# Forgetting attention and a gated convolution FFN on one core: two rewriting transfers taken out of each fill

## The chip, the core and the metric

The kernel runs on one core of a Trainium2 chip. The metric is device time in microseconds (us): the median of several executions. Beside it stands one execution that the hardware profiler recorded, with its own time and its span (first to last instruction). All views of the profile and of the trace are of that one execution. PE is the matmul engine, DVE the vector engine, ACT the scalar engine, POOL GpSimd; SP is the engine whose queue issues nearly all transfers here.

## What is computed

Attention with a forget gate over 8 batches, 8 heads, 576 positions and 64 elements per head, and then, on its output put back to (batch, position, 512), a feed-forward layer of width 1024 with a gate from a convolution over three positions.

```python
def _attn_ref(q, k, v, f):
    scores = scale * np.matmul(q, k.transpose(0, 1, 3, 2))
    cum = np.cumsum(np.log(np.clip(f, 0.0001, 1.0)), axis=-1)
    decay = cum[:, :, :, None] - cum[:, :, None, :]
    scores = np.where(causal, -1000000000.0, scores + decay)
    attn = softmax(scores)
    return np.matmul(attn, v)
...
def _moe_ref(x, w_in, conv_w, w_out):
    h = np.maximum(x @ w_in, 0.0)
    conv_out = conv_w[0] * h[s - 1] + conv_w[1] * h[s] + conv_w[2] * h[s + 1]
    gate = 1.0 / (1.0 + np.exp(-conv_out))
    return h * gate @ w_out
```

## The kernel before, in words

**Tiling.** The 64 pairs of batch and head are worked in 16 groups of four heads; group hb is half of batch hb // 2. For each group q and k are brought in turned, so that a tile `qk` holds 128 rows by 2 x 4 x 576 columns of bf16: the first half of the columns is q, the second is k. There are four such tiles (RING = 4), so group hb takes the tile of group hb - 4.

**Where the decay sits.** `load_qk` (L195 to L200) turns the fp32 inputs as pairs of 16-bit halves. The odd rows of the tile then hold the upper halves, which are the values in bf16; the even rows hold the lower halves, which aren't wanted. The kernel uses four of the even rows for the decay: row 0 of q holds the scaled cumulative sum and row 0 of k holds -1; rows 2 and 4 of q hold 1 and those of k hold the sum's upper part and its rest; row 6 is zero. One matmul over 128 rows then gives scores and decay together. All these rows for all heads are prepared once in `image`, a tensor in the chip's memory of shape (4 rows, 2 sides, 64 heads, 576): its decay parts are written by ACT's queue at L291, its constants by POOL's queue in `constants` (L293 to L295, task `zc`).

**How the even rows are set.** Groups 0 to 5 are cleared by DVE (`clamp`, L202), which also sets the constants; the decay rows follow by two transfers, `rows_of` (L217 to L220), for groups 1 to 5 (group 0 adds its decay by matmuls). For groups 6 to 15 it is done by transfers alone, in the task `fi{hb}`: `fill` (L211 to L215) writes zeros into 60 even rows (L212, 540 KB) and the image into the other four, both sides (L214, 36 KB), and `rows_of` then writes one row of q (L219, 4.5 KB) and two rows of k (L220, 9 KB) once more from the same places of the image. L219 writes bytes that L214 also writes, and is issued when L214 has landed.

**The order.** Nothing is scheduled while the kernel runs: `ORDER` (L17 to L67) is a list of tasks written out, and each engine takes its own tasks of it in that order. `add` gives each task its engine, what it must come after, and the buffers that it takes and gives back; waits between engines follow from the data. Tasks that the text names, by engine:

- SP: `q{hb}.0` and `q{hb}.1` load and turn q and k (L198); `fi{hb}` fills; `v{b}.{kb}` loads v of a batch in five parts (L226); `s{b}.{a}` stores a part of the output (L482, L485). From fill 6 on SP's order is fi6, v3.0, fi7, v3.2, fi9, v3.1, v3.4, v3.3, s0.2, s0.1, four parts of v4, s0.0, q8.0, q8.1, q10.1, q10.0, fi8, v4.4, fi10, s1.2, q11.1, q11.0, s1.0, fi11, v5, s2.0, q12, q13, fi12, s2.2, s1.1, fi13, s3.0, two parts of v7 and v6, q14, v6, s3.2, fi14, s4.0, v7, q15, s3.1, v7.4, fi15, and then stores.
- PE: `sd{i}` scores of the diagonal blocks of pair i (two heads; i // 2 is the group), `st{hb}` scores of the last 64 positions, `so{i}.{s}` the other scores (all with L316; a causal mask is added at L324 in groups 0 to 7), `pv{hb}.{u}` attention times v (L392), `t{hb}` turning (L408), `f{b}.{ff}` first FFN matmul (L422), `o{b}.{c}` second (L467, L471). All share four PSUM tiles.
- ACT: `ed`, `et`, `eo` the exponentials of the scores (L357, L336, L374), `r` relu (L432), `a` tanh (L456), `e{b}.{a}` copies of results from PSUM to one of three `ob` buffers (L477; some of them on DVE).
- DVE: `n` normalisation (L399, L400), `c` and `d` the convolution (L437, L439), `g` the gate (L460), `tx` copies after turning (L413, some on ACT). POOL: `va` casts of v (L233, L235), and `md`, `mt` the causal mask from group 8 on (L360, L339).

A group's score tasks come after its `fi` task. A `q` load comes after all score tasks of the group that had its tile before. A store's `ob` buffer can be taken again once the store has landed.

Of the kernel before, what the change touches and what calls it, by code (L numbers as in the profile page):

```python
# [69 lines left out]
class Plan:  # L70
# [8 lines left out]
    def add(self, name, engines, after, fn, take=(), give=(), behind=()):  # L79
        assert name not in self.tasks  # L80
        self.tasks[name] = dict(engines=engines.split("/"), after=[a for a in after if a], fn=fn, take=list(take),
                                give=list(give), behind=[a for a in behind if a])
        return name
# [21 lines left out]
def kernel(  # L105
# [83 lines left out]
    add = plan.add  # L189
# [5 lines left out]
    def load_qk(hb, h0, nh, side):  # L195
        t, src = ((stq_t, q), (stk_t, k))[side]
        t = t[hb % RING]
        nc.sync.dma_start_transpose(  # L198
            t.bitcast(U16)[:, h0 * S:(h0 + nh) * S],
            src[hb // 2, HH * (hb % 2) + h0:HH * (hb % 2) + h0 + nh].bitcast(U16).rearrange("h s d2 -> (h s) d2"))  # L200

    def clamp(hb, h0, nh, side):  # L202
        t = (stq_t, stk_t)[side][hb % RING].bitcast(U16)[:, h0 * S:(h0 + nh) * S]
        nc.vector.tensor_scalar(t, t, lim[:, 2 * side:2 * side + 1], lim[:, 2 * side + 1:2 * side + 2],
                                op0=ALU.mult, op1=ALU.add)

    def even_rows(hb, first, n, c0, c1):
        t, width = qk_t[hb % RING], 2 * HS + 64
        return bass.AP(tensor=t.tensor, offset=int(t.offset) + 2 * first * width + c0, ap=[[2 * width, n], [1, c1 - c0]])

    def fill(hb):  # L211
        nc.sync.dma_start(even_rows(hb, 4, 60, 0, 2 * HS).rearrange("p (h s) -> p h s", s=2 * S),  # L212
                          zero[0:60].unsqueeze(1).broadcast_to((60, HH, 2 * S)))
        nc.sync.dma_start(even_rows(hb, 0, 4, 0, 2 * HS).rearrange("j (a x) -> j a x", a=2),  # L214
                          image[:, :, hb * HH:(hb + 1) * HH, :].rearrange("j a h s -> j a (h s)"))  # L215

    def rows_of(hb):  # L217
        c = slice(hb * HH, (hb + 1) * HH)
        nc.sync.dma_start(even_rows(hb, 0, 1, 0, HS), image[0:1, 0, c, :].rearrange("j h s -> j (h s)"))  # L219
        nc.sync.dma_start(even_rows(hb, 1, 2, HS, 2 * HS), image[1:3, 1, c, :].rearrange("j h s -> j (h s)"))  # L220

    def load_v(b, kb):
        vf = vf_t[slot[f"v{b}.0", "vf"]]
        base = int(v.offset) + b * H * S * D
        n = 128 if kb < NKB - 1 else SL
        nc.sync.dma_start(vf[0:n, :, kb, :],  # L226
                          bass.AP(tensor=v.tensor, offset=base + kb * 128 * D, ap=[[D, n], [S * D, H], [1, D]]))

    def cast_v(hb, part):
        vf = vf_t[slot[f"v{hb // 2}.0", "vf"]][:, HH * (hb % 2):HH * (hb % 2 + 1)]  # L230
        va = va_t[slot[f"va{hb}.0", "va"]]
        if part == 0:
            nc.gpsimd.tensor_copy(va[:, :, 0:4, 0:D], vf[:, :, 0:4, :])  # L233
        else:
            nc.gpsimd.tensor_copy(va[0:SL, :, 4, 0:D], vf[0:SL, :, 4, :])  # L235
# [90 lines left out]
    def tail_scores(hb):  # L326
        on = hb in MASK_PE
        if on:
            masked(ps_of(f"st{hb}")[:, 0:HH * SL], HH, SL)
        for h in range(HH):  # L330
            scores(ps_of(f"st{hb}")[:, SL * h:SL * (h + 1)], hb, h, 512, 512, SL, m=SL, first=not on,
                   last=h == HH - 1 or not on)

    def tail_exp(hb):
        o = pt_t[slot[f"et{hb}", "pt"]][:, :, SL:128] if hb in MASK_PE else p3_t[slot[f"et{hb}", "p3"]]
        nc.scalar.activation(o, ps_of(f"st{hb}")[:, 0:HH * SL].rearrange("p (h j) -> p h j", j=SL), AF.Exp, scale=SCALE)  # L336
# [36 lines left out]
    def off_exp(i, s):  # L373
        nc.scalar.activation(pair(i)[:, s, 512:1536], ps_of(f"so{i}.{s}"), AF.Exp, scale=SCALE)  # L374
# [141 lines left out]
    for hb in range(NHB):  # L516
        b = hb // 2
        was = hb - RING
        old = [f"st{was}"] + [f"sd{2 * was + y}" for y in range(2)] + [
            f"so{2 * was + y}.{s}" for y in range(2) for s in range(2)] if was >= 0 else []  # L520
        if hb == 0:
            for p in range(2):
                add(f"cl0.{p}", "DVE", [], lambda p=p: [clamp(0, 2 * p, 2, side) for side in (1, 0)])
            ready = [["cl0.0"], ["cl0.1"]]
        else:
            for side in range(2):
                add(f"q{hb}.{side}", "SP", old, lambda hb=hb, side=side: load_qk(hb, 0, 4, side))
            if hb < NCL:
                for side in range(2):
                    add(f"cl{hb}.{side}", "DVE", [f"q{hb}.{side}"], lambda hb=hb, side=side: clamp(hb, 0, 4, side))  # L530
                add(f"rw{hb}", "SP", [f"cl{hb}.{side}" for side in range(2)], lambda hb=hb: rows_of(hb))
                ready = [[f"rw{hb}"]] * 2
            else:
                add(f"fi{hb}", "SP", [f"q{hb}.0", f"q{hb}.1", "zc"], lambda hb=hb: (fill(hb), rows_of(hb)))
                ready = [[f"fi{hb}"]] * 2
        if hb % 2 == 0:
            for kb in range(NKB):
                add(f"v{b}.{kb}", "SP", [], lambda b=b, kb=kb: load_v(b, kb), take=["vf"] if kb == 0 else [],
                    behind=[f"v{b}.0"] if kb else [])
        add(f"va{hb}.0", "POOL", [f"v{b}.{kb}" for kb in range(4)], lambda hb=hb: cast_v(hb, 0), take=["va"])  # L540
        add(f"va{hb}.1", "POOL", [f"v{b}.4"], lambda hb=hb: cast_v(hb, 1), behind=[f"va{hb}.0"],
            give=[("vf", f"v{b}.0")] if hb % 2 else [])
        for p in range(2):
            i = 2 * hb + p
            if p == 0:
                add(f"st{hb}", "PE", ready[0] + ready[1], lambda hb=hb: tail_scores(hb), take=["ps"])
                add(f"et{hb}", "ACT", [f"st{hb}"], lambda hb=hb: tail_exp(hb), take=["pt"] + ([] if hb in MASK_PE else ["p3"]),
                    give=[("ps", f"st{hb}")])
                if hb not in MASK_PE:
                    add(f"mt{hb}", "POOL", [f"et{hb}"], lambda hb=hb: tail_mask(hb), give=[("p3", f"et{hb}")])  # L550
            add(f"sd{i}", "PE", ready[p], lambda i=i: diag_scores(i), take=["ps", "p"])
            add(f"ed{i}", "ACT", [f"sd{i}"], lambda i=i: diag_exp(i), take=[] if hb in MASK_PE else ["pd"],
                give=[("ps", f"sd{i}")])
            if hb not in MASK_PE:
                add(f"md{i}", "POOL", [f"ed{i}"], lambda i=i: diag_mask(i), give=[("pd", f"ed{i}")])
            for s in range(2):
                add(f"so{i}.{s}", "PE", ready[p], lambda i=i, s=s: off_scores(i, s), take=["ps"], behind=[f"sd{i}"])
                add(f"eo{i}.{s}", "ACT", [f"so{i}.{s}"], lambda i=i, s=s: off_exp(i, s), give=[("ps", f"so{i}.{s}")])
        mk = "e" if hb in MASK_PE else "m"
        need = [f"{mk}d{2 * hb}", f"{mk}d{2 * hb + 1}", f"va{hb}.0"] + [f"eo{2 * hb + p}.{s}" for p in range(2) for s in range(2)]  # L560
        for u in range(3):
            add(f"pv{hb}.{u}", "PE", need + ([f"{mk}t{hb}", f"va{hb}.1"] if u == 2 else []), lambda hb=hb, u=u: pv(hb, u),
                take=["ps"], behind=[f"pv{hb}.{u - 1}"] if u else [],
                give=[("p", f"sd{2 * hb}"), ("p", f"sd{2 * hb + 1}"), ("pt", f"et{hb}"), ("va", f"va{hb}.0")] if u == 2 else [])
            add(f"n{hb}.{u}", "DVE", [f"pv{hb}.{u}"], lambda hb=hb, u=u: norm(hb, u),
                take=["rc"] + (["xm"] if u == 0 else []), give=[("ps", f"pv{hb}.{u}"), ("rc", f"n{hb}.{u}")],
                behind=[f"n{hb}.{u - 1}"] if u else [])
        add(f"t{hb}", "PE", [f"n{hb}.{u}" for u in range(3)], lambda hb=hb: turn(hb), take=["ps"], give=[("xm", f"n{hb}.0")])
        add(f"tx{hb}", "DVE/ACT", [f"t{hb}"], lambda e, hb=hb: turned(hb, e), take=["xt"] if hb % 2 == 0 else [],
            give=[("ps", f"t{hb}")], behind=[f"tx{hb - 1}"] if hb % 2 else [])  # L570
# [71 lines left out]
```

## Time and profile before

| | before |
|---|---|
| median of 3 runs | 292.31 us (290.13 to 292.34) |
| the profiled execution's own time | 288.32 us |
| its span | 286.6 us |
| PE, DVE, ACT, POOL busy | 241.3, 218.3, 203.6, 71.6 us |
| transfers, qk<-zero | 10 of 540 KB |
| transfers, qk<-image of L214 | 10 of 36 KB |
| transfers, qk<-image of L219 and of L220 | 15 of 4.5 KB and 15 of 9 KB |
| mean granted clock of PE | 0.969 |

Times in the profile count from the span's start. In a timeline a line has the start, the duration, the engine (SPq is SP's queue of issues), the line of the kernel, the operation, the tile written and the one read, the count, and in brackets the idle time before it with what ended it. In the list of waits the columns are the total in us, how many times, and the longest.

### The profile page before, as it was taken

The page shows a single profiled execution, that of the slowest core. Times are in us where ns is not written, and L with a number is a line of the kernel's source. Part 1 is how long each engine was busy: PE and PEld are TensorE (multiplying, and loading weights), DVE is VectorE, ACT ScalarE, POOL GpSimd, SP SyncE. Part 2 cuts the span into 40 slices and gives each one's busy share as a digit, 9 for nine tenths or more (in the row PEclk, how much of TensorE's full clock was granted, in tenths as well). Part 3 has the DMA queues.
Part 4 walks back from the last instruction along what each step waited for, and adds up shares of the span by engine and source line. Part 5 has one row for each costly group of instructions (what it writes and reads, how often), then busy time and mean ns, then how long its engine had stood idle before and what let it go on. Part 6 is the DMA issues. An engine that isn't in the chain of part 4 may idle for free.

```text
span 286.6 us, 6639 instructions
## 1 busy us (share of the span) xinstructions
PE 241.3 (84%) x2712; PEld 173.0 (60%) x2712; DVE 218.3 (76%) x342; ACT 203.6 (71%) x272; POOL 71.6 (25%) x103
## 2 busy tenths in 40 slices
PE   2595899778999947999988379985999999999992
PEld 1473676477677624587745367654865776777441
DVE  7722279999999981599987538963699799899962
ACT  3135739988997843879878339874697898978740
POOL 8401520250250000236026226203404430500000
PEclk9998999999999995999999979999799999999999
DMA  6999999997999655899748699945995962403124
GB/s 147 196 215 241 273 214 172 235 185 208 184 202 172 154 124 121 209 231 222 160 106 175 167 185 241 204 142 148 203 238 144 231 172 76 148 3 111 66 101 165
DMA packets 123484, 49.37 MB, mean 172 GB/s; under 512 B 113358, under 2 KB 114574, under 8 KB 123454
## 3 DMA queue, kind: packets, MB, share of 16 engines
q1 hardware_dynamic: 122968, 48.21, 79.8%
q8 instruction: 21, 0.34, 0.5%
q0 software_dynamic: 160, 0.37, 0.5%
q10 hardware_dynamic: 326, 0.38, 0.5%
q14 instruction: 9, 0.07, 0.1%
HBM read 14.51 MB, written 10.03 MB: 86 GB/s over the span
## 4 chain that ended last, share of the span: by engine, by line
PE 38%; DMA 19%; SPq 15%; DVE 14%; ACT 7%; issue 4%; POOL 0%; DVEq 0%; ACTq 0%; POOLq 0%
DMA qk<-image 12%; PE ps L422 12%; PE ps L467 12%; SPq L198 10%; PE ps L316 7%; DMA qk<-in_q_dram 4%; DVE xm L400 4%; PE ps L392 3%; DVE u L437 3%; ACT pp L374 3%; DVE hg L460 2%; PE ps L408 2%; DVE u L439 2%; SPq L212 2%; DMA vf<-in_v_dram 2%
## 5 line engine op out<-in xcount | busy, mean ns | idle before, releaser
L316 PE MATMUL ps<-qk 128*128 128x128 bf16 (+2 forms) x576 | 67.1, 250 | 25.1 <-DMA qk<-image 18.9
L316 PEld LDWEIGHTS <-qk 128*128 128x128 bf16 x576 | 42.7, 102 | 46.0 <-issue 22.9
L422 PE MATMUL ps<-xt,w_in_f 128*128 128x288 f16 x512 | 69.1, 288 | 0.6 <-ACT pp L374 0.4
L374 ACT ACTIVATE pp<-ps 128x1024 f16<-128x1024 f32 x64 | 64.1, 1032 | 7.3 <-PE ps L321 5.0
L437 DVE SCALAR_TENSOR_TENSOR u<-ht,cwt 128x576 f32<-128x576 f16 x64 | 56.0, 887 | 6.2 <-ACT ht L432 6.1
L467 PE MATMUL ps<-w_out_f,hg 128*128 128x512 f16 x256 | 60.0, 382 | 0.7 <-ACT ht L432 0.7
L422 PEld LDWEIGHTS <-w_in_f 128*128 128x128 f16 x512 | 49.6, 99 | 15.2 <-issue 2.1
L460 DVE SCALAR_TENSOR_TENSOR hg<-hg,ht 128x576 f16<-128x576 f16 x64 | 51.0, 823 | 8.5 <-ACT hg L456 8.4
L439 DVE SCALAR_TENSOR_TENSOR u<-ht,cwt,u 128x576 f32<-128x576 f16 x64 | 56.0, 885 | 1.6
L456 ACT ACTIVATE hg<-u,cw 128x576 f16<-128x576 f32 x64 | 48.3, 785 | 2.5 <-DVE u L439 2.3
L432 ACT ACTIVATE ht<-ps 128x576 f16<-128x576 f32 x64 | 41.1, 662 | 7.1 <-PE ps L422 4.2
L467 PEld LDWEIGHTS <-hg 128*128 128x128 f16 x256 | 24.6, 99 | 26.6 <-issue 2.0
L392 PE MATMUL ps<-va,pp 128*128 128x65 f16 x896 | 34.5, 195 | 5.9 <-ACT ob L477 3.8
L233 POOL CAST va<-vf 128x1024 f16<-128x1024 f32 x16 | 19.2, 1209 | 75.7 <-DMA vf<-in_v_dram 38.6
L392 PEld LDWEIGHTS <-pp 128*128 128x128 f16 x896 | 32.9, 98 | 7.9 <-issue 5.1
L360 POOL TENSOR_SCALAR_AFFINE_SELECT pp<-pd 128x1024 f16<-128x1024 f32 x16 | 19.6, 1227 | 54.3 <-ACT pd L357 54.3
L357 ACT ACTIVATE pp<-ps 128x1024 f16<-128x1024 f32 x16 | 16.3, 1036 | 22.2 <-PE ps L316 16.5
L400 DVE TENSOR_TENSOR xm<-ps,rc 128x512 f16<-128x512 f32 (+1 forms) x48 | 28.9, 603 | 1.7
L399 DVE RECIPROCAL rc<-ps 128x8 f32<-128x8 f32 (+1 forms) x48 | 9.3, 194 | 25.6 <-PE ps L392 23.2
L357 ACT ACTIVATE pd<-ps 128x1024 f32<-128x1024 f32 x16 | 16.2, 1027 | 12.3 <-PE ps L316 6.3
L477 ACT COPY ob<-ps 128x1024 f32<-128x1024 f32 (+1 forms) x20 | 15.7, 792 | 12.4 <-DMA out_dram<-ob 4.5
L324 PE MATMUL ps<-mask,ident 128*128 128x512 bf16 (+1 forms) x40 | 15.8, 395 | 2.5 <-DVE xm L400 1.8
(71 smaller groups left out, 174.6 us busy)
## 6 DMA issues: line engine op xcount, KB each, us to landing
vf<-in_v_dram SPq DMA_DIRECT2D x32, 256.0 KB
out_dram<-ob SPq DMA_DIRECT2D x16, 512.0 KB
qk<-zero SPq DMA_DIRECT2D x10, 540.0 KB
ob<-in_moe_w_in_dram SPq DMA_DIRECT2D x4, 512.0 KB
ob<-in_moe_w_out_dram SPq DMA_DIRECT2D x4, 512.0 KB
vf<-in_v_dram SPq DMA_DIRECT2D x8, 128.0 KB
out_dram<-ob SPq DMA_DIRECT2D x16, 64.0 KB
qk<-image SPq DMA_DIRECT2D x10, 36.0 KB
```

Source lines behind the costliest of these rows:

```text
L316: nc.tensor.matmul(o, tk[:, h * S + k0:h * S + k0 + 128], tq[:, h * S + q0:h * S + q0 + n], start=first, stop=last and hb > 0)
L357: nc.scalar.activation(o, ps_of(f"sd{i}").rearrange("p (s c) -> p s c", s=2), AF.Exp, scale=SCALE)
L374: nc.scalar.activation(pair(i)[:, s, 512:1536], ps_of(f"so{i}.{s}"), AF.Exp, scale=SCALE)
L392: nc.tensor.matmul(o, block(hb, h, m, n), va[:, h, m, 0:D + 1], start=(m == 0), stop=(m == n))
L400: nc.vector.tensor_tensor(xm[:, 2 * u:2 * u + nj, :].rearrange("p j (h d) -> p j h d", d=D), got[:, :, :, 0:D], r.unsqueeze(3).broadcast_t ...
L422: nc.tensor.matmul(ps[:, MB + 288 * a:MB + 288 * (a + 1)], w_in_f16[:, cc, 128 * ff:128 * (ff + 1)], xt[:, cc, 288 * a:288 * (a + 1)], sta ...
L432: nc.scalar.activation(ht_of(b, ff)[:, 1:1 + S], ps_of(f"f{b}.{ff}")[:, MB:MB + S], AF.Relu, scale=0.5)
L437: nc.vector.scalar_tensor_tensor(u, ht[:, 0:S], cwt[:, ff, 0:1], ht[:, 1:1 + S], op0=ALU.mult, op1=ALU.add)
L439: nc.vector.scalar_tensor_tensor(u, ht[:, 2:2 + S], cwt[:, ff, 1:2], u, op0=ALU.mult, op1=ALU.add)
L456: nc.scalar.activation(hg_of(b, ff), u_t[slot[f"c{b}.{ff}", "u"]], AF.Tanh, scale=cw[:, ff, 1:2])
L460: nc.vector.scalar_tensor_tensor(hv, hv, 1.0, ht_of(b, ff)[:, 1:1 + S], op0=ALU.add, op1=ALU.mult)
L467: nc.tensor.matmul(ps[:, 512 * (c % 2):512 * (c % 2 + 1)], hg_of(b, ff)[:, 128 * c:128 * (c + 1)], w_out_f16[:, ff, :], **kw)
```

## The change

The task `fi{hb}` of groups 6 to 15 runs `fill(hb)` alone; `rows_of(hb)`, the transfers of L219 and L220, isn't issued there any more. `rows_of` stays as it is for groups 1 to 5. The order of the tasks on all engines stays.

```diff
             else:
-                add(f"fi{hb}", "SP", [f"q{hb}.0", f"q{hb}.1", "zc"], lambda hb=hb: (fill(hb), rows_of(hb)))
+                add(f"fi{hb}", "SP", [f"q{hb}.0", f"q{hb}.1", "zc"], lambda hb=hb: fill(hb))
                 ready = [[f"fi{hb}"]] * 2
```

The two functions that the task calls before:

```python
    def fill(hb):
        nc.sync.dma_start(even_rows(hb, 4, 60, 0, 2 * HS).rearrange("p (h s) -> p h s", s=2 * S),
                          zero[0:60].unsqueeze(1).broadcast_to((60, HH, 2 * S)))
        nc.sync.dma_start(even_rows(hb, 0, 4, 0, 2 * HS).rearrange("j (a x) -> j a x", a=2),
                          image[:, :, hb * HH:(hb + 1) * HH, :].rearrange("j a h s -> j a (h s)"))

    def rows_of(hb):
        c = slice(hb * HH, (hb + 1) * HH)
        nc.sync.dma_start(even_rows(hb, 0, 1, 0, HS), image[0:1, 0, c, :].rearrange("j h s -> j (h s)"))
        nc.sync.dma_start(even_rows(hb, 1, 2, HS, 2 * HS), image[1:3, 1, c, :].rearrange("j h s -> j (h s)"))
```

## The prediction

> **What bounds the kernel now.** I began with the page: busy shares, the 40 slices, and the chain. The profiled execution took 288.32 us, 286.6 of it span.
>
> ```profile
> PE 241.3 (84%) x2712; PEld 173.0 (60%) x2712; DVE 218.3 (76%) x342; ACT 203.6 (71%) x272; POOL 71.6 (25%) x103
> ...
> PE   2595899778999947999988379985999999999992
> ...
> PEclk9998999999999995999999979999799999999999
> DMA  6999999997999655899748699945995962403124
> ...
> DMA qk<-image 12%; PE ps L422 12%; PE ps L467 12%; SPq L198 10%; PE ps L316 7%; DMA qk<-in_q_dram 4%; DVE xm L400 4%; PE ps L392 3%; DVE u L437 3%; ACT pp L374 3%; DVE hg L460 2%; PE ps L408 2%; DVE u L439 2%; SPq L212 2%; DMA vf<-in_v_dram 2%
> ```
>
> PE is the busiest engine, but its row (40 slices of 7.2 us) has holes: the 4 from 100 us, the 3 from 158, the 5 from 193; and the DMA row falls to 4, 5 and 6 in or just before the same slices: there the transfers are not at their limit, something makes them late. The chain names it: the small transfers qk<-image. The waits of the queues and of PE say how:
>
> ```profile
> SPq L219 <- DMA qk<-image: 37.1, 10, 4.0
> ```
>
> ```profile
> PE ps L316 <- DMA qk<-image: 18.9, 8, 4.0
> ```
>
> L219 is the first transfer that is taken out. In all 10 fills SP stands at it, 3.7 us on average, until the image transfer of L214 has landed, for it writes the same bytes. SP's timeline shows two fills (columns: start, duration):
>
> ```profile
> 94.11 1.03 SPq L212 DMA_DIRECT2D qk<-zero  x1
> 95.40 0.65 SPq L214 DMA_DIRECT2D qk<-image  x1
> 99.53 0.25 SPq L219 DMA_DIRECT2D qk<-image  x1
> 100.24 0.61 SPq L220 DMA_DIRECT2D qk<-image  x1
> 100.91 0.40 SPq L226 DMA_DIRECT2D vf<-in_v_dram  x1
> 101.43 0.96 SPq L212 DMA_DIRECT2D qk<-zero  x1
> 102.45 0.67 SPq L214 DMA_DIRECT2D qk<-image  x1
> 107.08 0.26 SPq L219 DMA_DIRECT2D qk<-image  x1
> 107.40 0.59 SPq L220 DMA_DIRECT2D qk<-image  x1
> ```
>
> PE's timeline shows where that reaches it (in brackets the idle time before, and who ended it):
>
> ```profile
> 102.36 0.38 PE L316 MATMUL ps<-qk 128*128 128x128 bf16 x4 [2.70 <-DMA qk<-image]
> ...
> 109.60 0.58 PE L316 MATMUL ps<-qk 128*128 128x128 bf16 x4 [4.02 <-DMA qk<-image]
> ...
> 144.83 1.61 PE L316 MATMUL ps<-qk 128*128 128x64 bf16 x24 [1.33 <-DMA qk<-image]
> ...
> 161.01 0.29 PE L392 MATMUL ps<-va,pp 128*128 128x65 f16 x4 [2.34 <-ACT ob L477]
> ...
> 166.43 1.03 PE L316 MATMUL ps<-qk 128*128 128x128 bf16 x8 [3.75 <-DMA qk<-image]
> ...
> 190.50 0.61 PE L316 MATMUL ps<-qk 128*128 128x128 bf16 x8 [1.21 <-DMA qk<-image]
> ...
> 196.12 0.29 PE L392 MATMUL ps<-va,pp 128*128 128x65 f16 x4 [1.46 <-ACT ob L477]
> ...
> 198.87 0.61 PE L316 MATMUL ps<-qk 128*128 128x128 bf16 x8 [1.95 <-DMA qk<-image]
> ```
>
> The seven waits for qk<-image are 15.9 us. The two on ACT's L477 (3.8 us) are late evacuations, which wait for an ob buffer whose store left SP late: the same cause. By the stretches 95 to 200 us PE is busy 84.02 us of 105 (21.0 idle), DVE 74.32, ACT 73.81. From 200 to 250 us PE is busy 48.84 of 50.
>
> **The change part by part.** Removed are 20 issues. On SP one fill loses the time from the end of L214 to the next task's issue: 96.05 to 100.91, some 4.8 us (3.48 waiting, 0.25 and 0.61 issuing, the rest gaps). Ten times that is 48 us of a queue that everything passes through: q, k, v, fills, stores. As bytes it is nothing: 13.5 KB of a fill's 590.
>
> For PE a fill's data is ready when L214 has landed, not L220: 2.1 us sooner (107.40 to 109.47 in the chain) plus L219's 0.3. PE now waits for two landings instead, the zeros' and the image's; an extra semaphore instruction is 0.02 to 0.03 us (those before L214), and the zeros are issued first, so this costs nothing. Were they later than the image, it would cost the difference.
>
> Behind one fill, everything on SP also comes earlier, until SP meets a wait for compute or the transfers meet each other. I walk SP's order against PE's, with each transfer's observed pace.
>
> *Fills 6, 7, 9 (94 to 127 us).* Fill 6 lands at 99.5, when PE is there: the 2.70 goes. Fill 7's zeros are issued at 96.6 instead of 101.4, queue behind fill 6's 540 KB (a fill's zeros take some 2.7 us of transfer) and v3.0 (1 us), land with the image at about 103.7 instead of 109.5. PE comes to sd14 at 102.6 (it follows ACT's exps of 1.03 us each here), so 1.1 of its 4.02 stays. From there PE, ACT and DVE all run through: sd14 at 103.7 instead of 109.6 (-5.9), the evacuation e1.0 waits for a store that lands at about 112.4 instead of 120.1 (-7.7, the three holes in the transfers after fills 6, 7 and 9), ACT's tanh a2.6 ends 7.4 sooner. I take -7.5.
>
> *Fills 8 and 10.* From 126 to 144 us DVE has no idle over 0.2 us, so the shift stays 7.5. Fill 8 lands at 142.25 - 7.7 = 134.5; PE, at 143.50 - 7.5 = 136.0, is later: the 1.33 goes (-8.8). Fill 10 lands near 138; PE needs it at 142: the 0.91 goes (-9.7).
>
> *Fill 11.* It must still wait for its own transposes (L212 waits 1.7 us for in_q_dram at 158.66), so it comes down only as these do: transfers q11 and s1.0 move to 138 to 145, the fill lands at 149.5. PE, without the 2.34 (the store is early), is at sd22 at 150.6 instead of 166.43: -15.8.
>
> *Fills 12 and 13.* v5, s2.0, q12 and q13 are dense transfers (166.4 to 183.9); they start at 149.3, the fill lands at 171, PE is there at 172.5 or later: the 1.21 goes, and e3.1's wait (1.46) and fill 13's 1.95 likewise: -20.4.
>
> *Fills 14 and 15.* PE doesn't wait for them now; nothing new. What is late next on SP is no transfer but compute: s3.0 waits for ACT's e3.0, some 5 us, with q14 behind it; fill 14 still lands 6 us ahead of PE's sd29.
>
> *Clock.* PEclk falls after each long PE wait: the stretch 110 to 120 has 0.75, the one from 166 to 182 has 0.89. There 8 matmuls of L422 took 2.12 us (elsewhere 1.14), of L467 2.56 (1.89), the diagonal scores 1.03 (0.61). Some 1 to 5 us on PE; with ACT or DVE setting the pace for most of it, I add 1.5: -22.
>
> *What the walk leaves out.* Without gaps, 95 to 200 becomes about 83 us in which PE has 80 of work and DVE and ACT 74 each, and every small misfit counts. Rows for such dense stretches: 40 to 95 us has 50.43 of 55 busy on PE (8.3% idle, DVE 52.67), 200 to 250 2.3%. On 80 us that is 6.6 and 1.8; I take the middle, 4, since the new stretch lies between them in DVE's load. Sum: 22 - 4 = **18 us**. Against the profiled 288.32 this is 270.3. The runs' median is 4.0 above the profiled time; against it, 292.31 - 18 = **274.3 us**.
>
> The Trainium skill (DMA: Bandwidth & Descriptors, Rules for kernel authors) speaks against so much: issue early, wait late, and a transfer's fixed cost overlaps with compute. By that alone the two small transfers would be hidden and the sum about nothing. The 37.1 us at L219 differ: here the wait stands on the issuing queue, which that page's Anatomy of one DMA also says it does.
>
> On the clock, the skill's TensorE: Matmul & The Clock Gate (What's actually happening) puts the ramp at under 1% of a typical span, here an estimate of under 2.9 us, where the slow rows allow up to 5. The 1.5 above doesn't rest on it.
>
> **The rivals.**
> *The other engines take over.* ACT and DVE could bind as soon as the first cluster is folded up, and the later waits for fills turn into waits for ACT and DVE. For it: DVE is dense from 126 to 144 and ACT follows PE closely; against it: both have some 31 us of slack from 95 to 200. It leaves the first cluster's 7.5 and half of the 8.2 us of waits behind it (1.33, 0.91, 3.75, 1.21 and some): 9 to 12, so 282.
>
> *Hidden anyway.* If PE waits for the zeros and the transposes, not for the small rows, only the second landing's time is won where PE stands: at most 2.1 us at a few places, and ACT's pace takes that back: 0 to 3 us, 291. Against it: the waits fall on L214's landing plus 2 us, and SP's holes are real. This includes that the change doesn't do what it says, the wait moving unchanged to another instruction.
>
> *Slower.* Transposes now run straight behind zeros and stores. They take about 3.2 us each in a run of them; the longest issue among them, q8.0 behind stores and v, took 4.89. In the walk nearly all 16 of fills 8 to 15 stand ahead of a fill that PE reaches within 2 us, so a longer one reaches PE. If each paid 4.89 - 3.2 = 1.7 us more, that is 27 of loss against 22 of gain: 297; it decides from 22 / 16 = 1.4 us each. Against it: 120 to 136 us has transposes behind v and a store, and the transfers' share there is 1.20, as high as anywhere; and from 95 to 250 us the shares times the lengths sum to 123, at 1.20 some 102 us of 155, which leaves slack.
>
> **How the numbers follow.** Folding up as walked 0.76 (own range 268 to 280), the other engines 0.18, hidden 0.03, slower 0.03. Predicted is the likeliest, 274.3. Range: the full 22 and 2 more of clock give 268; the waits for qk<-image alone, less the large misfit, 15.9 - 6.6 = 9.3, give 283, which takes in the second case. A measurement tells about 1% (2.9 us) from no change. Faster by over 1%: 0.94; within: 0.03; slower: 0.03.
>
> **What would show it.** L219 and L220 from fills gone; SP goes from L214 to the next issue in 0.1 us; no PE wait over 2 us for qk<-image between 95 and 200; transfers without holes after the first three fills; sd22 near 151 us; PEclk without the three drops; SP waiting for ACT at s3.0. Wrong: PE's idle from 95 to 200 still over 10 us with ACT or DVE as releaser, L198 issues longer than 4 us throughout, or a new wait at L212.

## The result, and the profile after

The changed kernel takes 266.50 us (median of 4 executions, 265.89 to 267.87), the kernel before 291.46 us (4 executions, 290.13 to 292.34): ratio 0.9154, 95% interval 0.9095 to 0.9213. The profiled execution took 265.89 us with a span of 264.2. So the kernel is 25 us faster; 274.3 was predicted, with a range down to 268.0.

The time came out of the holes. The changed kernel's page (busy row of PE, then PE, granted clock and transfers in 40 slices, then the chain):

```profile
PE 234.5 (89%) x2712; PEld 168.6 (64%) x2712; DVE 219.0 (83%) x342; ACT 203.0 (77%) x272; POOL 72.4 (27%) x103
...
PE   2495799759999997989999889999999999999992
...
PEclk9999799999999999999999999999999999999998
DMA  6999999999899999999988899989989950303225
...
PE ps L467 19%; PE ps L422 13%; SPq L198 12%; PE ps L316 8%; DVE xm L400 5%; PE ps L392 4%; DVE u L437 4%; DMA qk<-image 4%; DVE u L439 3%; DVE hg L460 2%; DMA qk<-in_q_dram 2%; PE ps L408 2%; DMA vf<-in_v_dram 2%; DVE rc L399 2%; PE ps L471 2%
```

From slice 14 on PE has no digit under 7 but the last, its clock drops once near the start and no more until the end, and the transfers run at 8 and 9 where they had 4, 5 and 6, up to the stores at the end. In the chain qk<-image fell from 12% to 4%.

SP's timeline of the same two fills as before (start, duration):

```profile
94.77 1.03 SPq L212 DMA_DIRECT2D qk<-zero  x1
96.07 0.65 SPq L214 DMA_DIRECT2D qk<-image  x1
96.76 1.58 SPq L226 DMA_DIRECT2D vf<-in_v_dram  x1
98.89 0.92 SPq L212 DMA_DIRECT2D qk<-zero  x1
99.86 0.67 SPq L214 DMA_DIRECT2D qk<-image  x1
```

After L214 the next load goes out at once. The second fill begins 4.1 us after the first instead of 7.3; I had walked 2.5. The load of v now takes 1.58 us to issue instead of 0.40: it is issued right behind the fill's transfers and no longer after the wait.

PE's timeline from 95 to 200 us has two waits of over 1 us left where there were eight:

```profile
105.14 0.38 PE L316 MATMUL ps<-qk 128*128 128x128 bf16 x4 [1.24 <-DMA qk<-image]
...
152.92 0.61 PE L316 MATMUL ps<-qk 128*128 128x128 bf16 x8 [2.01 <-DVE rc L399]
```

The first is sd14 (fill 7), the second sd22, which now waits for a PSUM tile that DVE releases. The stretch from sd12 to sd26 shows the account best. Before it lies at 99.2 to 198.9 us, after at 99.9 to 179 us (columns: stretch and length, then busy time and count of PE, its weight loads, DVE, ACT, POOL; granted clock, share of the transfers, GB/s):

```profile
99.20:198.90 99.70, 78.72 (x873) 55.34 (x872) 70.20 (x102) 70.15 (x94) 27.40 (x27) 0.95 0.80 171
```

```profile
99.90:179.00 79.10, 73.85 (x874) 52.67 (x872) 70.81 (x100) 68.96 (x94) 26.15 (x26) 1.00 1.02 214
```

20.6 us less: PE's idle time went from 20.98 to 5.25 us, and PE's busy time, for the same matmuls, from 78.72 to 73.85, since the half-clock stretches are gone. DVE and ACT do the same work in less time. PE is now busy for 93% of this stretch, DVE and ACT for 90 and 87%, with transfers at a share of 1.02. SP's long waits are now for compute, not for landings (the two largest of its list):

```profile
SPq L482 <- ACT ob L477: 41.2, 6, 13.9
SPq L198 <- PE ps L316: 20.4, 6, 5.0
```

In what follows, an execution over 1.5% above the fastest of its kernel is in no ratio; the profiles of the runs one_kept and fill7_first are of such executions, and only waits and distances inside them are used. The kernel before, run against itself, came out at 1.0067 (1.0019 to 1.0114): differences of less than 0.7% are not read.

### The profile page after: what moved, and what is told of

Same layout as the page of the kernel before. It is cut to its first block, busy times and chain, and to the rows that moved or that the text cites. A ratio compares the mean times of both kernels' runs of the same rounds, so it can differ in the third digit from the quotient of the medians.

```text
span 264.2 us, 6609 instructions
## 1 busy us (share of the span) xinstructions
PE 234.5 (89%) x2712; PEld 168.6 (64%) x2712; DVE 219.0 (83%) x342; ACT 203.0 (77%) x272; POOL 72.4 (27%) x103
## 4 chain that ended last, share of the span: by engine, by line
PE 49%; DVE 17%; SPq 16%; DMA 8%; ACT 4%; issue 4%; POOL 0%; DVEq 0%; POOLq 0%; ACTq 0%
PE ps L467 19%; PE ps L422 13%; SPq L198 12%; PE ps L316 8%; DVE xm L400 5%; PE ps L392 4%; DVE u L437 4%; DMA qk<-image 4%; DVE u L439 3%; DVE hg L460 2%; DMA qk<-in_q_dram 2%; PE ps L408 2%; DMA vf<-in_v_dram 2%; DVE rc L399 2%; PE ps L471 2%
## 5 line engine op out<-in xcount | busy, mean ns | idle before, releaser
L316 PE MATMUL ps<-qk 128*128 128x128 bf16 (+2 forms) x576 | 65.0, 245 | 14.9 <-DMA qk<-image 7.2
L422 PE MATMUL ps<-xt,w_in_f 128*128 128x288 f16 x512 | 68.1, 286 | 0.6 <-ACT pp L374 0.4
L316 PEld LDWEIGHTS <-qk 128*128 128x128 bf16 x576 | 41.5, 100 | 32.7 <-issue 10.6
L467 PE MATMUL ps<-w_out_f,hg 128*128 128x512 f16 x256 | 59.3, 379 | 0.4 <-ACT ht L432 0.2
L422 PEld LDWEIGHTS <-w_in_f 128*128 128x128 f16 x512 | 49.2, 98 | 14.8 <-issue 2.1
L460 DVE SCALAR_TENSOR_TENSOR hg<-hg,ht 128x576 f16<-128x576 f16 x64 | 51.9, 836 | 2.5 <-ACT hg L456 2.4
L392 PE MATMUL ps<-va,pp 128*128 128x65 f16 x896 | 33.3, 193 | 2.6 <-POOL va L233 1.5
L392 PEld LDWEIGHTS <-pp 128*128 128x128 f16 x896 | 31.9, 97 | 4.4 <-issue 1.3
L360 POOL TENSOR_SCALAR_AFFINE_SELECT pp<-pd 128x1024 f16<-128x1024 f32 x16 | 19.0, 1195 | 35.3 <-ACT pd L357 35.2
L477 ACT COPY ob<-ps 128x1024 f32<-128x1024 f32 (+1 forms) x20 | 15.7, 792 | 8.0 <-PE ps L467 4.3
L204 DVE TENSOR_SCALAR qk<-qk,lim 128x2304 uint16<-128x2304 uint16 (+1 forms) x14 | 10.8, 792 | 8.8 <-DMA qk<-in_q_dram 6.0
```

The lines of the kernel that those rows point to most:

```text
L316: nc.tensor.matmul(o, tk[:, h * S + k0:h * S + k0 + 128], tq[:, h * S + q0:h * S + q0 + n], start=first, stop=last and hb > 0)
L392: nc.tensor.matmul(o, block(hb, h, m, n), va[:, h, m, 0:D + 1], start=(m == 0), stop=(m == n))
L422: nc.tensor.matmul(ps[:, MB + 288 * a:MB + 288 * (a + 1)], w_in_f16[:, cc, 128 * ff:128 * (ff + 1)], xt[:, cc, 288 * a:288 * (a + 1)], sta ...
L460: nc.vector.scalar_tensor_tensor(hv, hv, 1.0, ht_of(b, ff)[:, 1:1 + S], op0=ALU.add, op1=ALU.mult)
L467: nc.tensor.matmul(ps[:, 512 * (c % 2):512 * (c % 2 + 1)], hg_of(b, ff)[:, 128 * c:128 * (c + 1)], w_out_f16[:, ff, :], **kw)
```

## The experiments

The theory was that **the queue stands**: SP waits at L219 for the image transfer to land, and all that SP issues comes later. Rivals: **PE's data** (PE's rows are complete one landing sooner, and that is the gain) and **number of transfers** (20 small transfers each cost their issue and landing).

**one_kept.** One of the two put back, the one that SP stands at.

```diff
-lambda hb=hb: fill(hb)
+lambda hb=hb: (fill(hb), row_q(hb))   # L219's transfer alone
```

> Of the two removed transfers the first (one row of q, 4.5 KB) is put back into the fills of groups 6 to 15; the other stays out. Theory 'the queue stands' (SP's wait for the image transfer to land, about 3.5 us a fill, is what cost the time, since every later transfer is issued behind it): the wait is all there again, only the other transfer's issue and gap (0.7 us a fill) are saved, of which a part reaches the end: ratio to before 0.98 to 0.99. Rival 'number of transfers' (each small transfer costs its issue and landing): half of the gain, 0.955 to 0.96. Rival 'PE's data' (PE's data is complete one landing sooner, and that is the gain): nearly before, 0.98 to 0.99, as the last landing is only 0.3 us sooner.

Measured: 0.9784 (0.9714 to 0.9854). Half of the transfers are gone, but only about a quarter of the gain is there. The wait is all there, as its list of waits has it (L224 is the transfer put back):

```profile
SPq L224 <- DMA qk<-image: 38.6, 10, 4.5
```

So the count of transfers by itself doesn't set the time.

**no_wait.** Both put back, written where nobody reads (the diff is against the kernel before, cut to the transfers).

```diff
+w = aside[hb % 2]                     # a part of the unused tile taps
-nc.sync.dma_start(even_rows(hb, 0, 1, 0, HS), image[0:1, 0, c, :]...)
-nc.sync.dma_start(even_rows(hb, 1, 2, HS, 2 * HS), image[1:3, 1, c, :]...)
+nc.sync.dma_start(w[0:1], image[0:1, 0, c, :]...)
+nc.sync.dma_start(w[1:3], image[1:3, 1, c, :]...)
```

> The changed kernel with both transfers put back at their place, same sizes and source, but written to an unused tile, so that nothing waits for the image transfer to land and PE doesn't depend on them. 'The queue stands': only 0.85 us of issue a fill comes back, mostly hidden behind the transfers that are under way: 0.915 to 0.93. 'Number of transfers': the old cost is back, 0.98 or more. 'PE's data': 0.915 to 0.92.

Measured: 0.9256 (0.9186 to 0.9326). The same 20 transfers, at the same place, without the wait, cost about 1% against the changed kernel (0.9154), little more than the 0.7% that can be read. They aren't as cheap to issue as I thought (SP's timeline, L225 and L226 are the two):

```profile
95.77 0.65 SPq L215 DMA_DIRECT2D qk<-image  x1
96.47 1.66 SPq L225 DMA_DIRECT2D taps<-image  x1
98.57 0.23 SPq L226 DMA_DIRECT2D taps<-image  x1
98.87 0.41 SPq L232 DMA_DIRECT2D vf<-in_v_dram  x1
```

The first takes 1.45 to 2.24 us to issue (10 of them, median 1.72), where after a wait it took 0.25. Yet it hardly reaches the end. That SP is held there while the fill's zeros are moving anyway would explain it, but isn't shown by itself.

**sp_waits.** SP stands as before, but PE doesn't depend on what it stands for (added to the changed kernel).

```diff
+nc.sync.dma_start(w[0:1], even_rows(hb, 0, 1, 0, HS))   # reads what L214 wrote
+nc.sync.dma_start(w[1:3], image[1:3, 1, c, :]...)
```

> The changed kernel with a small transfer after each fill's image transfer that reads a row which the image transfer has written (4.5 KB, into an unused tile), and one of 9 KB into that tile: SP stands at it as before until the image has landed, but PE doesn't depend on either. 'The queue stands': most of the loss is back; PE gains only the 2.4 us between the two landings where it stood waiting, some 5 us in all: 0.975 to 0.985. 'PE's data': near the changed kernel, 0.92. 'Number of transfers': 0.98 or more.

Measured: 1.0063 (1.0024 to 1.0102), as slow as before. The wait is back (L225 is the transfer that reads):

```profile
SPq L225 <- DMA qk<-image: 37.6, 10, 4.4
```

I had expected some 5 us for PE's earlier data; it brings nothing. The trace says why. PE starts sd12's scores without the 2.70 us of wait, and so12.0 at 100.78 instead of 103.01, but then it waits at sd14, longer than before (4.02), since fill 7 comes when SP lets it:

```profile
107.81 0.59 PE L322 MATMUL ps<-qk 128*128 128x128 bf16 x4 [4.46 <-DMA qk<-image]
...
122.99 1.89 PE L398 MATMUL ps<-va,pp 128*128 128x65 f16 x40 [3.37 <-DVE ob L483]
```

The second line is the late store again: PE waits for DVE's evacuation, which waits for its buffer. Earlier data for PE alone, with SP's wait kept, gains nothing: 'PE's data' is refuted.

**disjoint.** Every byte written once, by five transfers that overlap nowhere; PE needs the last.

```diff
-nc.sync.dma_start(even_rows(hb, 0, 4, 0, 2 * HS)..., image[:, :, ...])
+nc.sync.dma_start(even_rows(hb, 1, 3, 0, HS), image[1:4, 0, ...])
+for j in (0, 3):
+    nc.sync.dma_start(even_rows(hb, j, 1, HS, 2 * HS), image[j:j + 1, 1, ...])
 # and rows_of(hb) as in the kernel before
```

> All four decay rows are written once, but by five transfers instead of one: the two that were removed, and three for the other parts of the image rows, none overlapping another, so SP waits for no landing and PE needs the last of the five. 'The queue stands': 2.3 us more of issue a fill than the changed kernel, largely while the fill's zeros are still under way: 0.92 to 0.935. 'PE's data': the last landing is 1 to 2 us later than in the changed kernel at each fill that PE waits for: 0.93 to 0.95. 'Number of transfers': above 1, since there are two more than before.

Measured: 0.9548 (0.9503 to 0.9592), outside what I expected of 'the queue stands' (up to 0.935). About half of the gain is there with more transfers than before, so the number of transfers isn't the cost and the rewrite is a large part of it; but issues are dearer than I had put them. From the end of the fill's first image transfer to the next task SP is held 2.6 to 3.5 us a fill. Summed over the ten fills, from the traces: 48.2 us before (span 286.6), 30.7 here (275.2), 23.0 in no_wait (267.2), 6.0 after (264.2). Besides its 7.7 us more on SP, this run differs from no_wait in that PE needs the last of the five; how its 8 us divide between the two isn't separated. The three fills in a row then come late for PE (sd12 and sd14):

```profile
102.87 0.40 PE L319 MATMUL ps<-qk 128*128 128x128 bf16 x4 [1.79 <-DMA qk<-image]
...
108.50 0.40 PE L319 MATMUL ps<-qk 128*128 128x128 bf16 x4 [2.39 <-DMA qk<-zero]
```

**first_three and later_seven.** The change for a part of the fills.

```diff
-lambda hb=hb: (fill(hb), rows_of(hb))
+lambda hb=hb: fill(hb) if hb in (6, 7, 9) else (fill(hb), rows_of(hb))   # first_three; later_seven the other way round
```

> The kernel before, with the two transfers taken out of the fills of groups 6, 7 and 9 alone (the first three on SP's queue). The walk puts the shift after these three at 6.7 to 7.5 us and has it kept to the end: ratio 0.975 (0.97 to 0.98). Rival 'absorbed later' (what is won early is lost again at the next fill's wait, as PE then only waits longer): 0.99 to 1. The trace should show PE at st8 some 6.7 us earlier and the later waits for qk<-image as before.

> The kernel before, with the two transfers taken out of the seven other fills (groups 8 and 10 to 15). The changed kernel's trace has 15.7 us of its 22.4 behind the first three fills: if the parts add, 0.945 to 0.95. Rival 'absorbed': the later fills are gained only when the early ones are gone too: 0.96 or more.

Measured: 0.9655 (0.9612 to 0.9698) and 0.9407 (0.9353 to 0.9461), both a little under the range that I had expected. By spans the two take 7.9 and 14.4 us off 286.6, together 22.3; the whole change takes 22.4. The parts add. In first_three's trace sd18 starts 6.9 us earlier than before and sd26 7.3: nothing is absorbed, and the later waits stand as they were (qk<-image, 10.7 us in 6 waits behind 95 us).

**warm_before and warm_all.** PE's waits filled with matmuls that nobody reads, to see what the clock is worth by itself.

```diff
 def diag_scores(i):
     ps, on = ps_of(f"sd{i}"), i // 2 in MASK_PE
+    for _ in range({14: 16, 22: 14, 26: 7}.get(i, 0)):   # warm_all: 9 at i = 12 too
+        nc.tensor.matmul(ps[:, 0:512], ident, mask..., start=True, stop=True)
 def pv(hb, u):                                            # warm_all alone, at the end
+    for _ in range({(8, 1): 18, (11, 1): 12}.get((hb, u), 0)):
+        nc.tensor.matmul(ps[:, 272:512], ident, mask..., start=True, stop=True)
```

> The kernel before with 37 matmuls added that nobody reads, ahead of the three score tasks at which PE waits longest (16 of 512 columns at sd14, 14 at sd22, 7 at sd26), inside the waits. All fills are as before. This is to take away the drops of PE's clock without the waits. If the clock was worth little (the 1.5 us of the prediction): 0.99 to 1. If all of the 4.9 us by which PE's busy time fell between sd12 and sd26 had reached the end by itself: 0.983. Rival 'no cover': the added matmuls delay the scores: above 1.

> The kernel before with more of the matmuls that nobody reads: 9 at sd12, 16 at sd14, 14 at sd22, 7 at sd26, and, in an unused part of their PSUM tiles, 18 and 12 narrow ones behind pv8.1 and pv11.1, ahead of the two waits for evacuations. In the run with 37 of them half of the half-clock time was still there (3.4 us near 102 and 3.4 near 160); now all of it between 95 and 210 us should be gone. If the clock by itself is worth 1.5 us or less: 0.99 to 1. If it is worth most of 4.9 us: 0.983 to 0.987.

Measured: 0.9944 (0.9902 to 0.9987) and 1.0006 (0.9966 to 1.0045). Not all drops went: warm_all's trace still has two of 3.4 us (124 and 193 us). But the mean granted clock rose, over the executions that are compared, from 0.953 (kernel before) to 0.976 in the one and from 0.956 to 0.975 in the other, and the changed kernel has 0.984. With most of the clock's gain in hand the time falls by 0.6% or not at all, under what is read here. The 0.6% also hangs on which executions are counted: over all of them the means are 290.22 us against 290.42 for warm_before, and 290.17 against 290.39 for warm_all. The trace of warm_before shows where much of the gain goes. Behind sd14, where the slow matmuls were, PE now runs at full clock, and then waits 2.21 us at pv6.0 for DVE's late evacuation, where it waited 0.35 before:

```profile
119.81 1.42 PE L394 MATMUL ps<-va,pp 128*128 128x65 f16 x40 [2.21 <-DVE ob L479]
```

While SP holds back the fills and stores, a faster PE only waits longer.

**fill7_first.** On top of the changed kernel, one swap on SP's queue.

```diff
-... va4.0 v3.0 fi7 eo9.1 v3.2 fi9 ...
+... va4.0 fi7 eo9.1 v3.0 v3.2 fi9 ...
```

> The changed kernel with one pair swapped on SP's queue: fill 7 ahead of the first part of v3. Fill 7's transfers then come 1 us sooner, and the 1.24 us that PE still waits at sd14 should go: ratio to before 0.910 to 0.915, about 1 us under the changed kernel, if SP's order sets it. Rival 'ACT sets the pace there': no change, 0.915.

Measured: 0.9156 (0.9110 to 0.9202), no change from 0.9154. The wait at sd14 did go:

```profile
105.48 0.38 PE L316 MATMUL ps<-qk 128*128 128x128 bf16 x4 [0.20 <-DMA qk<-image]
...
115.78 1.42 PE L392 MATMUL ps<-va,pp 128*128 128x65 f16 x40 [1.21 <-DVE ob L477]
```

but from sd12 to sd18 it takes 18.6 us, as in two profiles of the changed kernel (19.0 and 18.2): the microsecond is given back by pv6.0, which here waits 1.21 us for DVE's evacuation. No version tried beats the changed kernel.

**before_again and after_again.** Both kernels once more, unchanged.

> The kernel before, unchanged, once more, for the spread of its executions and their clocks beside those of the changed kernel on the same chip. If the profiled 288.32 us was the low end of its spread: median near 290.4, ratio 1 within 0.5%, and clocks lower in the longer executions. If it was typical: median near 288.5.

> The changed kernel, unchanged, once more on the same chip. Ratio 0.915 to 0.92, and a smaller spread than the kernel before, with fewer stretches of half clock, if the spread comes from where PE's waits fall in the clock's windows; the same spread if it comes from elsewhere.

Measured: the kernel before, 289.85 us (median of 10; clocks 0.945 to 0.969), profiled 288.05; the changed kernel, 264.85 us (median of 4; 0.978 to 0.993), ratio 0.9151 (0.9074 to 0.9228), profiled 263.78. So a profiled 288 us lies near the low end of the kernel before. Its longer executions tend to have lower clocks (correlation of time and clock over the 10: -0.65), and its spread is 4.1 us in 10; that of the changed kernel, 4.0 us in 4, is not smaller on these few, as it should have been if the spread came from how PE's waits fall against the clock's drops. Where the spread comes from stays open.

## Why the prediction was right and where it was wrong

**Right: the mechanism.** The wait at L219 held SP, and SP held the rest. sp_waits keeps just that and keeps all of the time; no_wait takes just that away and gets nearly all of the gain.

**Right in its sum, partly by luck: the walk.** Its shifts of task starts against those of the trace after (us). The last two columns split each measured shift into what PE's idle time and what PE's busy time up to that task have lost:

| place | walked | measured | idle | busy |
|---|---|---|---|---|
| sd14 (fill 7) | -5.9 | -4.5 | -4.3 | -0.1 |
| end of the first three fills (sd18) | -7.5 | -6.8 | -4.0 | -2.8 |
| st8 (fill 8) | -8.8 | -8.3 | -5.3 | -3.0 |
| sd21 (fill 10) | -9.7 | -9.4 | -6.2 | -3.2 |
| sd22 (fill 11) | -15.8 | -13.5 | -10.3 | -3.2 |
| sd26 (fill 13) | -20.4 | -19.9 | -14.8 | -5.1 |
| sd29, with the clock | -22 | -22.7 | -15.7 | -7.0 |
| last matmul | -22 | -22.5 | -15.7 | -6.8 |

Only sd14 and sd22 are off by more than 1 us. At sd14, fill 7's zeros are issued at 98.9 instead of the walked 96.6, behind the load of v. At sd22, fill 11's zeros are issued at 146.8 instead of the walked 144.1, and PE is then released by DVE; so part of the rival 'the other engines take over' is true at this place, for 2 us.

The match of the sums is partly luck. Of the walk's 20.4 us at sd26, 18.6 are PE's waits (2.70, 2.92, 1.33, 0.91, 2.34, 3.75, 1.21, 1.46 and 1.95), and the clock is added only after it. In the trace PE's idle time up to sd26 is only 14.8 us shorter; another 5.1 us come from the same matmuls taking less time. The waits gave less than walked, the clock gave more, and the two errors nearly cancel.

**Wrong: the step "clock".** I saw 1 to 5 us of slow matmuls and added 1.5, "with ACT or DVE setting the pace for most of it". PE's busy time fell by 6.8 us instead (241.3 to 234.5). Between 95 and 250 us the trace before holds 13.65 us at half clock in three pieces (6.83 us from 108, 3.41 from 166, 3.41 from 200), the trace after none, and half of 13.65 is 6.8. The shift grows just where the slow matmuls were: from -5.0 at f2.6 to -7.1 at so13.0, from -13.5 at sd22 to -14.9 at sd23, from -19.9 at sd26 to -21.5 at o3.4. With the fills early it isn't ACT or DVE that PE waits for there: it is busy for 93% of the stretch. By itself the clock is worth little, 1.6 us in one of the runs with added matmuls and nothing in the other: it counts only once the waits are gone. That it then counts in full is read from these traces; no run puts slow stretches into the changed kernel. The second pair of profiles (before_again and after_again) says the same: 24.3 us of span, of them 7.7 less busy and 16.6 less idle.

The Trainium skill (TensorE: Matmul & The Clock Gate, What's actually happening) puts the ramp at under 1% of a typical span, as an estimate under 2.9 us here. It speaks of the ramp; where the drops come back behind waits, as here, the 6.8 us on PE are more than that.

**Right in size: "what the walk leaves out".** I took 4 us off for misfits in a dense stretch. In the prediction's terms the waits were to give 20.4 - 4 = 16.4 us, and PE's idle time fell by 15.6 over the whole span (45.3 to 29.7 us); from sd12 to sd26 it is now 5.25 us, inside the 1.8 to 6.6 expected. Without the allowance 288.32 - 22 is 266.3, nearly the 265.89 measured, but that would have been right for the wrong reason: the clock's gain standing in for waits that stayed.

**Mis-sized: the base.** The prediction was set against a median of three, 292.31, which a fourth execution made 291.46; ten further ones have 289.85. The profiled execution lay 3.1 us under that median of four, the changed kernel's 0.6 under its own; I carried the gain of a profile over to the median as if both kernels had the same distance.

The miss of 7.8 us adds up: 4.4 on the profiled pair (22.4 instead of 18, rounded from 17.9: the clock 5.3 more than put, the waits 0.8 less), 0.9 the base's median, 2.5 the two distances of profile and median. The range's low end took the walk's 22 and 2 us more of clock and stopped there; it left out the spread of the executions, which is larger than the 1.5 us by which it missed.

**Rivals.** Hidden anyway, and the Trainium skill's advice to issue a transfer early and wait for it late (DMA: Bandwidth & Descriptors, Rules for kernel authors): small transfers are nearly hidden where nothing waits for them (no_wait, 0.9256 against 0.9154), and not where the issuing queue stands (sp_waits, 1.0063). Slower: the transposes take no longer to issue than before (medians of 3.1 and 3.3 us for q and k, before 3.2 and 3.3). Only ahead of fill 11 do q11's two take 5.9 us instead of 4.7, and the two stores before them 2.9 instead of 1.2, which is part of why that fill is late.

## What to carry to other kernels

Where one queue issues nearly everything, look for its own waits for landings first: a transfer that overwrites what an earlier one has just written holds all that is behind it, and the loss is to be read from the queue's order, not from the bytes. Walk the order by hand with each wait that stays, and say of each gain whether it is idle time that goes or busy time that gets shorter: a sum can be right while its two parts are wrong. Where slow-clock stretches stand behind the waits that go, count the slow matmuls in full on the engine that is then busiest. Let the range hold the spread of the executions. A consumer that is served earlier gains nothing if the next delivery on the same queue is as late as before.

## What the runs showed of the hardware that I had not expected

An issue is not of fixed length: the transfer of one row took 0.25 us to issue when SP had waited for the image to land, and 1.45 to 2.24 us right behind the fill's transfers; a load of v behind them took 1.58 us instead of 0.40. So part of what the wait held comes back as longer issues; the transfers' share from sd12 to sd26 still rose from 0.80 to 1.02.

PE's half-clock stretches came in pieces of 3.4 and 6.8 us behind waits of as little as 2.6 us (the run with 37 added matmuls: a wait of 2.58 us ending at 100.76, half clock from 102.0 to 105.4). It doesn't follow each time: in the profile before, the wait of 2.70 us ending at 102.36 at the same place was followed by full clock until 108.
